# A fused attention, expert and gated network: the gated weights' preparation cut into three jobs, a step apart, behind the step's main operations

## The chip, the cores and the metric

The kernel runs on one core of a Trainium2 chip. The metric is the device time of one execution in microseconds (us); less is better. Given are three plain runs and one profiled execution of the kernel before.

## The reference

Three layers follow each other, all in float32 (shortened):

```python
# 1. attention with exponential features: 4 batches, 8 heads, 576 tokens, 64 wide
q_p, k_p = phi(q), phi(k)          # exp(+-(proj - max|proj|)), 2 x 128 features
x = (q_p @ (k_p.T @ v)) / (q_p @ sum(k_p) + 1e-6)      # then 2304 x 512
# 2. experts: 8, one for each token (the largest logit), gate weight = its softmax
h = np.maximum(x[mask] @ w1[e], 0.0)                   # 512 -> 1024
out[mask] = gate_w[mask, None] * (h @ w2[e])           # 1024 -> 512
# 3. gated layer: w_a, w_b 512 x 1536, w_out 1536 x 512
return (a * b @ w_out)             # a = x @ w_a, b = x @ w_b
```

The gated weights come to the device as 64-bit floats, each as two 32-bit words.

## The kernel before

The program is unrolled. A planner orders each engine's instructions when the program is built: it goes by priorities, by the dependencies and by its own costs for each operation. `high_priority(offset=-LOWP)` puts what is inside 200 places later in priority; `issue_after(ins)` lets what is inside follow `ins` on `ins`'s engine, in order and without a wait of its own. On the chip every engine runs its list in order, so an instruction that waits holds up all that is queued behind it. SyncE (SP) issues nearly all transfers, in order too.

The attention (class `Attn`) ends near 175 us in the profile. The expert stage (`Moe.run`) follows. The tokens come in two halves of 1152, each routed by itself (`Route`), and go in four tiles of 608 tokens. A tile has eight steps (`NJ`): in steps 0 to 3 two blocks each of the first layer (`l1`), in steps 4 to 7 one block each of the second (`l2`), so that the stage has 32 steps. TensorE multiplies each matrix in three products of high and low parts (`mm3`, L54 to L56), 304 columns at a time. An expert's weight block `s` is loaded, ScalarE rounds it to its high part `wh` (L552) and VectorE takes the low part `wl` (L553). Of the hidden layer ScalarE makes the high part `hh` (L591) and VectorE the low part `hl` (L592); both layers of matmuls need them, and the PSUM buffer of a block is free only when both have read it. GpSimd gathers token rows `xg` (L561), and TensorE turns them (`transp`).

At the start of step k, `run` calls what `side[k]` holds. Among it are the steps of the second half's routing (in steps 0, 2, 4, 8) and the preparation of ten of the twelve blocks of gated weights (`prep`, one block f at steps 3, 5, 8, 10, ... 25). The other two are prepared in the gated stage.

`prep` works on two halves of a block. For each half `narrow` loads the 64-bit words into `raw` (L688, two buffers), ScalarE takes the absolute value of the upper words (L692, tile `cvs`), GpSimd clamps it from below (L693), and VectorE builds the float32 in five instructions (L694 to L701) on `cvt`, `cvs` and, last, `wsum`. When both halves are there, VectorE makes four sums of column blocks (L710 to L713), ScalarE and VectorE split the block into a high part (`whi`, L718) and a low part (L719), in two cuts, and SyncE stores both in device memory (`wsc`, L720 and L721).

At step 28 `open_first` closes the pool of the preparation (`cctx`), opens in its room the pools of the gated stage, loads the first gated weights (`fw`, L730) and makes the first terms (`ysum`, `yl`). After the expert stage comes a branch that is not taken here, and then the gated stage (`Moe2.run`): 36 steps of seven products `abp` and six output accumulations each.

Of the kernel before, what the change touches and what calls it, by code (L numbers as in the profile page):

```python
# [48 lines left out]
def f32(ap):  # L49
    return ap.bitcast(F32)  # L50
# [283 lines left out]
class Route:  # L334
# [17 lines left out]
    def gate(self):  # L352
# [18 lines left out]
        ex = self.w([NG, E], "ex")  # L371
# [94 lines left out]
    def table(self):  # L466
# [19 lines left out]
        def lookup(name, col, n, row, parts):  # L486
            k = len(parts)
            hot = self.w([NG, n], name + "h", BF16)
            rhs = self.w([NG, k, n], name + "r", BF16)
# [30 lines left out]
class Moe:  # L520
# [26 lines left out]
    def splitw(self, T, j):  # L547
# [5 lines left out]
        nc.vector.tensor_sub(lo, src, f32(hi))  # L553
# [25 lines left out]
    def l1(self, T, f):  # L579
# [3 lines left out]
        for g in range(2):  # L583
            gs = slice(g * CG, g * CG + CG)
            for c in range(4):
# [5 lines left out]
        nc.scalar.activation(hh, ps[:, :, :CG], AF.Relu)  # L591
        nc.vector.scalar_tensor_tensor(out=hl, in0=ps[:, :, :CG], scalar=0.0, in1=f32(hh), op0=ALU.max,  # L592
                                       op1=ALU.subtract)
        T["h", f] = (hh, hl)

    def l2(self, T, m):
        nc = self.nc
        wh, wl = T["w", 4 + m]
        for g in range(2):
# [4 lines left out]
            nc.scalar.copy(self.y[T["rt"].bp][:, m, ds(T["s"][g], CG)], ps)  # L604
# [52 lines left out]
class Moe2:  # L657
# [14 lines left out]
    def pools(self, ctx, ps_a, ps_l):  # L672
# [3 lines left out]
        self.p_t[1] = pool("f_t1", 4)  # L676
# [4 lines left out]
    def narrow(self, pool, f, half, dst, nt):  # L681
        nc = self.nc
        n = 768
        if not self.f64:
            nc.sync.dma_start(out=dst, in_=self.w[f][:, n * half:n * half + n])
            return
        raw = pool.tile([P, n, 2], I32, tag="raw", name="raw", bufs=2)
        nc.sync.dma_start(out=raw.rearrange("p n w -> p (n w)"), in_=self.w[f][:, 2 * n * half:2 * n * half + 2 * n])  # L688
        lo, hi = raw[:, :, 0], raw[:, :, 1]
        t = pool.tile([P, n], I32, tag="t", name="cvt", bufs=nt)  # L690
        s = pool.tile([P, n], I32, tag="s", name="cvs", bufs=nt)
        nc.scalar.activation(s.bitcast(F32), hi.bitcast(F32), AF.Abs)  # L692
        nc.gpsimd.tensor_scalar(out=s.bitcast(F32), in0=s.bitcast(F32), scalar1=LEAST, scalar2=None, op0=ALU.max)  # L693
# [9 lines left out]
    def prep(self, f, pool, nw, nt):  # L703
        nc = self.nc
        w = pool.tile([P, 2304], F32, tag="w", name="wsum", bufs=nw)
        for half, c in enumerate((0, 1280)):
            self.narrow(pool, f, half, w[:, c:c + 768], nt)
# [6 lines left out]
        for x, y in self.CUTS:  # L714
# [6 lines left out]
            nc.sync.dma_start(out=self.wsc[f][1][:, x:y], in_=src)  # L721

# [169 lines left out]
def trn_kernel(ctx, tc, qk, v, vt, w_phi, mod_id, w_gate, bias, wm, wf, out):  # L892
# [37 lines left out]
    with ExitStack() as mctx:  # L930
# [27 lines left out]
        def conv(f):  # L958
            with tc.high_priority(offset=-LOWP):
                m2.prep(f, cv[0], 2, 2)  # L960

        K0, K1 = 3, len(tiles) * mo.NJ - 4
        for f in range(NPRE):
            side.setdefault(K0 + (K1 - K0) * f // NPRE, []).append(lambda f=f: conv(f))
# [90 lines left out]
```

## Time and profile before

| | us |
|---|---|
| plain runs: median (lowest to highest) of 3 | 829.94 (828.87 to 830.32) |
| profiled execution: time | 837.45 |
| profiled execution: span | 835.7 |
| TensorE busy in the span | 804.0 (96%) |
| VectorE busy | 595.1 (71%) |
| ScalarE busy | 373.8 (45%) |
| GpSimd busy | 140.4 (17%) |
| mean granted clock of TensorE | 0.991 |

The span goes from the first to the last instruction that the profile saw; the profiled execution's own time lies a little above it, and above the plain runs. Busy times are those of the profile's page; matmuls overlap, and their ends are modelled.

### The profile page before, as it was taken

Reading aid. Unit: us, or ns where it says so; the run is one execution under the profiler, and the core shown is the slowest. Engines: PE = TensorE matmul, PEld = TensorE weight load, DVE = VectorE, ACT = ScalarE, POOL = GpSimd, SP = SyncE. Lnnn points to the kernel's source line nnn. Section 1 sums busy time; section 2 is a strip of 40 time slices with the busy share of each in tenths; the row PEclk is TensorE's granted clock in tenths of the full one; section 3 lists DMA queues with packets and bytes.
Section 4 is the critical chain, followed back from the end, with each engine's and each line's share of the span. In section 5 each row is a group of like instructions: output and inputs, shape, how many; then the busy total and the mean of one; then the engine's idle time right before and its main releaser. Section 6 shows DMA issues by size and latency. Waiting matters only on the chain.

```text
span 835.7 us, 18329 instructions
## 1 busy us (share of the span) xinstructions
PE 804.0 (96%) x7283; PEld 755.5 (90%) x7284; DVE 595.1 (71%) x1071; ACT 373.8 (45%) x665; POOL 140.4 (17%) x164
## 2 busy tenths in 40 slices
PE   8999999889999999979999999999999999999996
PEld 6999888789999999979999899999999999999995
DVE  5888898589998999987488854775544676445553
ACT  3656555344544455453345433553333364333332
POOL 1000009342217433310021100030000002000002
PEclk9999999999999999999999999999999999999998
DMA  7666432466768888776499776576666568665632
GB/s 272 193 183 195 149 120 82 115 206 225 249 238 300 289 302 296 271 240 266 170 360 339 254 281 207 187 271 226 205 206 201 186 223 280 206 198 189 224 123 92
DMA packets 85163, 184.22 MB, mean 220 GB/s; under 512 B 27760, under 2 KB 37520, under 8 KB 85072
## 3 DMA queue, kind: packets, MB, share of 16 engines
q1 hardware_dynamic: 81872, 173.21, 61.4%
q0 software_dynamic: 3040, 9.72, 3.4%
q8 instruction: 58, 0.95, 0.5%
q14 instruction: 33, 0.27, 0.1%
q10 hardware_dynamic: 160, 0.07, 0.0%
HBM read 145.21 MB, written 37.75 MB: 219 GB/s over the span
## 4 chain that ended last, share of the span: by engine, by line
issue 44%; PE 4%; POOL 3%; POOLq 0%; ACT 0%
POOL out L800 2%; PE abp L54 1%; PE abp L56 1%; PE abp L55 1%; POOL cvs L693 1%; PE op L55 0%; PE op L54 0%; PE op L56 0%; POOLq L1052 0%; ACT cvs L692 0%; POOLq L800 0%; ACT pc L844 0%
## 5 line engine op out<-in xcount | busy, mean ns | idle before, releaser
L844 ACT COPY pc<-abp 128x384 f32<-128x384 f32 x252 | 120.6, 479 | 199.6 <-PE abp L56 195.9
L54 PE MATMUL abp<-yh,fw 128*128 128x384 f32 x504 | 170.1, 337 | 2.4 <-ACT pc L844 1.3
L56 PE MATMUL abp<-yh,fw 128*128 128x384 f32 x504 | 170.0, 337 | 0.0
L55 PE MATMUL abp<-yl,fw 128*128 128x384 f32 x504 | 169.8, 337 | 0.0
L54 PEld LDWEIGHTS abp<-yh,fw 128*128 128x128 f32 x504 | 94.6, 188 | 11.6 <-ACT pc L844 2.4
L55 PEld LDWEIGHTS abp<-yl,fw 128*128 128x128 f32 x504 | 94.7, 188 | 7.4
L693 POOL TENSOR_SCALAR cvs<-cvs 128x768 f32<-128x768 f32 x24 | 61.5, 2562 | 198.1 <-ACT cvs L692 184.4
L56 PEld LDWEIGHTS abp<-yh,fw 128*128 128x128 f32 x504 | 94.6, 188 | 0.0
L54 PE MATMUL hp<-mxh,wh 128*128 128x304 f32 x256 | 79.1, 309 | 7.9 <-DVE hl L592 6.8
L55 PE MATMUL op<-fw,gh 128*128 128x512 f32 x216 | 85.7, 397 | 0.0
L54 PE MATMUL op<-fw,gh 128*128 128x512 f32 x216 | 85.1, 394 | 0.0
L56 PE MATMUL op<-fw,gl 128*128 128x512 f32 x216 | 85.0, 394 | 0.0
L55 PE MATMUL yp<-hl,wh 128*128 128x304 f32 x256 | 77.3, 302 | 1.7 <-DVE hl L592 1.7
L55 PE MATMUL hp<-mxl,wh 128*128 128x304 f32 x256 | 78.2, 306 | 0.0
L56 PE MATMUL hp<-mxh,wl 128*128 128x304 f32 x256 | 77.8, 305 | 0.0
L56 PE MATMUL yp<-hh,wl 128*128 128x304 f32 x256 | 77.8, 304 | 0.0
L54 PE MATMUL yp<-hh,wh 128*128 128x304 f32 x256 | 76.9, 302 | 0.0
L800 POOL DMA_INDIRECT out<-o,perm x18 | 18.3, 1019 | 348.3 <-ACT o L799 341.2
L190 ACT ACTIVATE qts<-qtp 128x512 f32<-128x512 f32 (+1 forms) x80 | 38.3, 558 | 64.8 <-PE qtp L187 64.8
L855 DVE TENSOR_TENSOR d<-u,pc 128x768 f32<-128x768 f32 x36 | 34.5, 957 | 32.2 <-ACT pc L844 32.0
L54 PEld LDWEIGHTS hp<-mxh,wh 128*128 128x128 f32 x256 | 48.7, 190 | 9.4 <-issue 6.4
L156 DVE TENSOR_REDUCE m<-pjp 128x8 f32<-128x1024 f32 (+2 forms) x49 | 45.1, 933 | 12.0 <-PE pjp L154 12.0
(191 smaller groups left out, 1587.5 us busy)
## 6 DMA issues: line engine op xcount, KB each, us to landing
fw<-wsc SPq DMA_DIRECT2D x72, 512.0 KB, 5.4
fw<-wsc SPq DMA_DIRECT2D x144, 256.0 KB, 3.3
raw<-in_moe_w SPq DMA_DIRECT2D x24, 768.0 KB, 7.2
s<-in_moe_w SPq DMA_DIRECT2D x32, 512.0 KB, 4.2
fw<-wsc SPq DMA_DIRECT2D x72, 128.0 KB, 5.7
wsc<-whi SPq DMA_DIRECT2D x12, 640.0 KB, 4.3
wsc<-wsum SPq DMA_DIRECT2D x12, 640.0 KB, 6.8
wsc<-whi SPq DMA_DIRECT2D x12, 512.0 KB, 7.0
```

The source lines that it names most:

```text
L54: nc.tensor.matmul(out, lh, rh, start=start, stop=False)
L55: nc.tensor.matmul(out, lh, rl, start=False, stop=False)
L56: return nc.tensor.matmul(out, ll, rh, start=False, stop=stop).ins
L156: nc.vector.tensor_reduce(out=mv, in_=pv, op=ALU.max, axis=AX.X, apply_absolute_value=True)
L190: nc.scalar.activation(t[:, s, :n, :], ps[:, :n, :], AF.Exp, scale=1.0 - 2.0 * s)
L693: nc.gpsimd.tensor_scalar(out=s.bitcast(F32), in0=s.bitcast(F32), scalar1=LEAST, scalar2=None, op0=ALU.max)
L800: st = nc.gpsimd.indirect_dma_start(out=self.out[:, :], out_offset=bass.IndirectOffsetOnAxis(ap=self.routes[bp].perm[:, c:c + 1], axis=0), ...
L844: copied = nc.scalar.copy(x, ps).ins
L855: nc.vector.tensor_add(d, u, x.unsqueeze(1).to_broadcast([P, 2, n]))
```

## The change

The preparation is cut into three kinds of job. For each half of a block, `fetch` issues its raw transfer in step k, `clamp` lets ScalarE and GpSimd make `cvs` in step k + 1, and `narrow` lets VectorE build the float32 in step k + 2; behind the second half's `narrow` follow the sums, the split and the stores (`park`). Halves start at steps 2, 3, 4, 5, 6, 8, 9, ... 24, twenty of them, the gaps being 24/20 steps on average. All of a job is put behind the last main operations of the step before (`mo.act` on ScalarE: hh or the copy of the output; `mo.dve` on VectorE: hl or wl). `raw` has three buffers in place of two, `cvt` one in place of two. In the gated stage the two blocks left are prepared by the same jobs, a step apart, with two raw buffers as before. Room is found by sharing tags in the routing (`ex` with `bstmp`; the second half's `hot` and `rhs`) and by three in place of four buffers in `f_t1`.

```diff
         mx = self.w([NG], "mx")
         nc.vector.tensor_reduce(out=mx, in_=lg, op=ALU.max, axis=AX.X)
         nc.vector.tensor_sub(lg, lg, mx.unsqueeze(2).to_broadcast([P, NG, E]))
-        ex = self.w([NG, E], "ex")
+        ex = self.w([NG, E], "bstmp")
         nc.scalar.activation(ex, lg, AF.Exp)
         gt = self.gt = self.w([NG], "gt")
         nc.vector.tensor_reduce(out=gt, in_=ex, op=ALU.add, axis=AX.X)
...
 
         def lookup(name, col, n, row, parts):
             k = len(parts)
-            hot = self.w([NG, n], name + "h", BF16)
-            rhs = self.w([NG, k, n], name + "r", BF16)
+            hot = self.w([NG, n], "hot" if self.bp else name + "h", BF16)
+            rhs = self.w([NG, k, n], "rhs" if self.bp else name + "r", BF16)
             lhs = self.w([NG, P], "lhs" if self.bp else name + "l", BF16)
             onehot(hot, "icol", col, n)
             for i, v in enumerate(parts):
...
         hi = self.p_w.tile([P, 8, P], F32R, tag="h", name="wh")
         lo = self.p_w.tile([P, 8, P], F32R, tag="l", name="wl")
         nc.scalar.copy(hi, src)
-        nc.vector.tensor_sub(lo, src, f32(hi))
+        self.dve = nc.vector.tensor_sub(lo, src, f32(hi)).ins
         T["w", j] = (hi, lo)
 
     def gather(self, T, j):
...
                                 c == 0, c == 3)
         hh = self.p_h.tile([P, 2, CG], F32R, tag=f"h{f}", name="hh")
         hl = self.p_h.tile([P, 2, CG], F32R, tag=f"l{f}", name="hl")
-        nc.scalar.activation(hh, ps[:, :, :CG], AF.Relu)
-        nc.vector.scalar_tensor_tensor(out=hl, in0=ps[:, :, :CG], scalar=0.0, in1=f32(hh), op0=ALU.max,
-                                       op1=ALU.subtract)
+        self.act = nc.scalar.activation(hh, ps[:, :, :CG], AF.Relu).ins
+        self.dve = nc.vector.scalar_tensor_tensor(out=hl, in0=ps[:, :, :CG], scalar=0.0, in1=f32(hh), op0=ALU.max,
+                                                  op1=ALU.subtract).ins
         T["h", f] = (hh, hl)
 
     def l2(self, T, m):
...
             for f in range(8):
                 hh, hl = T["h", f]
                 self.last = mm3(nc, ps, wh[:, f, :], wl[:, f, :], hh[:, g, :], hl[:, g, :], f == 0, f == 7)
-            nc.scalar.copy(self.y[T["rt"].bp][:, m, ds(T["s"][g], CG)], ps)
+            self.act = nc.scalar.copy(self.y[T["rt"].bp][:, m, ds(T["s"][g], CG)], ps).ins
 
     def run(self, tiles, side={}):
         NT, NJ = len(tiles), self.NJ
...
         tc = self.tc
         pool = lambda n, b: ctx.enter_context(tc.tile_pool(name=n, bufs=b, side="right", reuse_waits="tile"))
         self.p_w[1] = pool("f_w1", 1)
-        self.p_t[1] = pool("f_t1", 4)
+        self.p_t[1] = pool("f_t1", 3)
         self.p_c = pool("f_c", 1)
         self.p_g = pool("f_g", 2)
         self.ps_a, self.ps_l = ps_a, ps_l
 
-    def narrow(self, pool, f, half, dst, nt):
+    def fetch(self, f, half, pool, n):
+        if not self.f64:
+            return None
+        c = 768 * 2
+        raw = pool.tile([P, 768, 2], I32, tag="raw", name="raw", bufs=n)
+        self.nc.sync.dma_start(out=raw.rearrange("p n w -> p (n w)"), in_=self.w[f][:, c * half:c * half + c])
+        return raw
+
+    def clamp(self, raw, pool, n):
+        if not self.f64:
+            return None
         nc = self.nc
-        n = 768
+        s = pool.tile([P, 768], I32, tag="s", name="cvs", bufs=n)
+        nc.scalar.activation(s.bitcast(F32), raw[:, :, 1].bitcast(F32), AF.Abs)
+        nc.gpsimd.tensor_scalar(out=s.bitcast(F32), in0=s.bitcast(F32), scalar1=LEAST, scalar2=None, op0=ALU.max)
+        return s
+
+    def narrow(self, f, half, raw, s, pool, w):
+        nc = self.nc
+        dst = w[:, 1280 * half:1280 * half + 768]
         if not self.f64:
-            nc.sync.dma_start(out=dst, in_=self.w[f][:, n * half:n * half + n])
+            nc.sync.dma_start(out=dst, in_=self.w[f][:, 768 * half:768 * half + 768])
             return
-        raw = pool.tile([P, n, 2], I32, tag="raw", name="raw", bufs=2)
-        nc.sync.dma_start(out=raw.rearrange("p n w -> p (n w)"), in_=self.w[f][:, 2 * n * half:2 * n * half + 2 * n])
         lo, hi = raw[:, :, 0], raw[:, :, 1]
-        t = pool.tile([P, n], I32, tag="t", name="cvt", bufs=nt)
-        s = pool.tile([P, n], I32, tag="s", name="cvs", bufs=nt)
-        nc.scalar.activation(s.bitcast(F32), hi.bitcast(F32), AF.Abs)
-        nc.gpsimd.tensor_scalar(out=s.bitcast(F32), in0=s.bitcast(F32), scalar1=LEAST, scalar2=None, op0=ALU.max)
+        t = pool.tile([P, 768], I32, tag="t", name="cvt")
         nc.vector.tensor_scalar(out=t, in0=s, scalar1=3, scalar2=0x3FFFFFF8,
                                 op0=ALU.logical_shift_left, op1=ALU.bitwise_and)
         nc.vector.scalar_tensor_tensor(out=t, in0=hi, scalar=-0x40000000, in1=t,
...
                                        in1=s.bitcast(F32), op0=ALU.mult, op1=ALU.mult)
         nc.vector.tensor_add(dst, t.bitcast(F32), s.bitcast(F32))
 
-    def prep(self, f, pool, nw, nt):
+    def sumw(self, pool, nw):
+        return pool.tile([P, 2304], F32, tag="w", name="wsum", bufs=nw)
+
+    def park(self, f, w, pool):
         nc = self.nc
-        w = pool.tile([P, 2304], F32, tag="w", name="wsum", bufs=nw)
-        for half, c in enumerate((0, 1280)):
-            self.narrow(pool, f, half, w[:, c:c + 768], nt)
         a11, a12, a21, s2, s1, a22 = (w[:, 256 * i:256 * i + 256] for i in range(6))
         s4 = w[:, 2048:]
         nc.vector.tensor_add(s1, a21, a22)
...
             nc.vector.tensor_sub(lo, src, f32(hi))
             nc.sync.dma_start(out=self.wsc[f][0][:, x:y], in_=f32(hi))
             nc.sync.dma_start(out=self.wsc[f][1][:, x:y], in_=src)
+
+    def jobs(self, f, pool, nw, nraw, ns):
+        st = {}
+
+        def fetch(half):
+            st["raw", half] = self.fetch(f, half, pool, nraw)
+
+        def clamp(half):
+            st["s", half] = self.clamp(st["raw", half], pool, ns)
+
+        def narrow(half):
+            if not half:
+                st["w"] = self.sumw(pool, nw)
+            self.narrow(f, half, st["raw", half], st["s", half], pool, st["w"])
+            if half:
+                self.park(f, st["w"], pool)
+
+        return fetch, clamp, narrow
 
     def weights(self, k):
         nc, f = self.nc, k % self.NF
...
         side = {k: [low(tc, rs[f])] for f, k in enumerate((0, 2, 4, 8))}
         side[9] = [close_work]
 
-        def conv(f):
-            with tc.high_priority(offset=-LOWP):
-                m2.prep(f, cv[0], 2, 2)
-
-        K0, K1 = 3, len(tiles) * mo.NJ - 4
+        def conv(f, half, job):
+            def run():
+                with tc.high_priority(offset=-LOWP), tc.issue_after(mo.act), tc.issue_after(mo.dve):
+                    job(half)
+            return run
+
+        K0, K1 = 2, len(tiles) * mo.NJ - 4
         for f in range(NPRE):
-            side.setdefault(K0 + (K1 - K0) * f // NPRE, []).append(lambda f=f: conv(f))
+            fetch, clamp, narrow = m2.jobs(f, cv[0], 2, 3, 2)
+            for half in range(2):
+                k = K0 + (K1 - 2 - K0) * (2 * f + half) // (2 * NPRE)
+                for i, job in enumerate((fetch, clamp, narrow)):
+                    side.setdefault(k + i, []).append(conv(f, half, job))
         ts, src0 = {}, []
 
         def first():
...
     cv.append(ctx.enter_context(tc.tile_pool(name="cv2", bufs=1, **tl)))
     side = {}
     for f in range(NPRE, Moe2.NF):
-        side.setdefault(2 * (f - NPRE), []).append(lambda f=f: m2.prep(f, cv[1], 1, 1))
+        for i, job in enumerate(m2.jobs(f, cv[1], 1, 2, 2)):
+            for half in range(2):
+                side.setdefault(2 * (f - NPRE) + i, []).append(lambda job=job, half=half: job(half))
     ps_l = ctx.enter_context(tc.tile_pool(name="ps_l2", bufs=2, space=PSUM, **tl))
     ps_a = ctx.enter_context(tc.tile_pool(name="ps_a2", bufs=1, space=PSUM, **tl))
     m2.pools(ctx, ps_a, ps_l)
```

## Rows read from the trace of the kernel before

**Rows 1.** Busy time by stretch (start:end, length; engine time and count; TensorE clock, DMA).

```profile
205.00:390.00 185.00, 176.89 (x1277) 175.35 (x1276) 165.98 (x264) 89.80 (x125) 60.71 (x26) 0.99 0.77 270
370.00:375.00 5.00, 1.42 (x8) 1.20 (x7) 5.00 (x7) 2.78 (x3) 0.00 (x0) 0.87 0.56 147
375.00:380.00 5.00, 5.00 (x31) 5.00 (x30) 4.48 (x6) 0.68 (x1) 0.00 (x0) 0.79 0.94 364
390.00:395.00 5.00, 5.00 (x38) 5.00 (x38) 4.55 (x6) 1.71 (x4) 0.00 (x0) 1.00 0.99 360
```

**Rows 2.** TensorE's timeline where it waited (start, length; idle before and releaser in brackets).

```profile
269.11 0.41 PE L55 MATMUL yp<-hl,wh 128*128 128x304 f32 x1 [1.74 <-DVE hl L592]
...
306.22 0.38 PE L54 MATMUL hp<-mxh,wh 128*128 128x304 f32 x1 [1.21 <-DVE hl L592]
...
360.32 0.41 PE L54 MATMUL hp<-mxh,wh 128*128 128x304 f32 x1 [1.58 <-DVE hl L592]
...
374.20 0.59 PE L54 MATMUL hp<-mxh,wh 128*128 128x304 f32 x1 [3.58 <-DVE hl L592]
...
410.20 0.44 PE L54 MATMUL abp<-yh,fw 128*128 128x384 f32 x1 [1.02 <-ACTq L983]
```

**Rows 3.** TensorE's waits from 415 us to the end.

```profile
PE abp L54 <- ACT pc L844: 1.3, 3, 0.8
```

**Rows 4.** VectorE's waits from 176 to 400 us.

```profile
DVE cvt L694 <- POOL cvs L693: 11.9, 5, 3.6
```

**Rows 5.** VectorE's timeline near three of TensorE's waits.

```profile
265.71 0.56 DVE L694 TENSOR_SCALAR cvt<-cvs 128x768 int32<-128x768 int32 x1 [3.56 <-POOL cvs L693]
...
350.83 0.56 DVE L694 TENSOR_SCALAR cvt<-cvs 128x768 int32<-128x768 int32 x1 [2.02 <-POOL cvs L693]
351.30 0.42 DVE L713 TENSOR_TENSOR wsum<-wsum 128x256 f32<-128x256 f32 x1
...
368.79 0.56 DVE L694 TENSOR_SCALAR cvt<-cvs 128x768 int32<-128x768 int32 x1 [2.45 <-POOL cvs L693]
...
373.28 1.48 DVE L592 SCALAR_TENSOR_TENSOR hl<-hp,hh 128x608 fp32r<-128x608 f32 x2
```

**Rows 6.** ScalarE's timeline before the longest wait.

```profile
365.64 0.91 ACT L692 ACTIVATE cvs<-raw 128x768 f32<-128x768 f32 x1 [5.94 <-DMA raw<-in_moe_w]
```

**Rows 7.** GpSimd's timeline, the clamp ahead of VectorE's wait at 265.71 us.

```profile
263.52 2.16 POOL L693 TENSOR_SCALAR cvs<-cvs 128x768 f32<-128x768 f32 x1
```

**Rows 8.** Transfers: issues, size, median us from issue to landing.

```profile
fw<-wsc SPq DMA_DIRECT2D x72, 512.0 KB, 5.4
...
raw<-in_moe_w SPq DMA_DIRECT2D x24, 768.0 KB, 7.2
```

**Rows 9.** SyncE's queue waits from 176 to 391 us.

```profile
SPq L688 <- DVE cvs L699: 18.9, 9, 5.7
```

**Rows 10.** Expert matmuls of the second layer: first and last start.

```profile
L54 PE MATMUL yp<-hh,wh x256: 296/300/391, 204.0 to 408.6; 128*128 128x304 f32 x128
```

**Rows 11.** VectorE's busy time 176 to 205 us on cvt, raw and wsum, in that order.

```profile
176.00:205.00 29.00, 9.35 (x13) 1.00 0.61 203
...
176.00:205.00 29.00, 5.68 (x6) 3.65 (x4) 1.00 0.61 203
...
176.00:205.00 29.00, 4.48 (x7) 1.06 (x1) 1.00 0.61 203
```

**Rows 12.** The rank of the second route: matmuls and the copy behind them.

```profile
L391 PE MATMUL rkp<-oh,ones x18: 166/188/203, 116.6 to 198.4; 128*128 128x72 bf16 x2, 128*128 128x64 bf16 x2, 128*128 128x56 bf16 x2, 128*128 128x48 bf16 x2
...
L394 DVE COPY R<-rkp x2: 226/233/240, 117.0 to 203.1; 128x80 f32<-128x80 f32 x2
```

**Rows 13.** VectorE's timeline: an instruction and the one that reads its result.

```profile
278.35 0.94 DVE L696 SCALAR_TENSOR_TENSOR cvt<-raw,cvt 128x768 int32<-128x768 int32 x1
279.32 0.56 DVE L698 TENSOR_SCALAR cvs<-cvt 128x768 int32<-128x768 int32 x1
```

**Rows 14.** SyncE's timeline: the first gated weights' loads.

```profile
391.84 20.56 SPq L730 DMA_DIRECT2D fw<-wsc  x13
```

## The prediction

> **What bounds the kernel now.** I first read the busy time by stretch, to see where TensorE can still gain anything. The change lives in the expert stage, which lies between about 176 and 410 us. In 205 to 390 us TensorE is busy 176.9 of 185 us and VectorE 166.0 [rows 1]. TensorE sets the pace, but VectorE is so full that one bad wait of its own is enough to hold TensorE up. The second view is TensorE's timeline at the places where it stood still: four times in this stretch, 1.74, 1.21, 1.58 and 3.58 us, together 8.1 us, and each time the releaser is hl, the low part of the hidden layer, which VectorE makes [rows 2]. The third is VectorE's list of waits: 11.9 us in five waits for GpSimd's clamp cvs [rows 4]. The timelines join the two: VectorE waits 3.56, 2.02 and 2.45 us for a clamp shortly before TensorE's waits at 269, 360 and 374 us; in the last case the two hl that TensorE needs start only at 373.28 [rows 5]. One step further back ScalarE, which feeds the clamp, had idled 5.94 us for the transfer raw [rows 6]. So the chain to read is transfer, ScalarE, GpSimd, VectorE, TensorE.
>
> After the longest wait the granted clock is 0.87 and 0.79 of full speed (2.4 GHz being full) for ten microseconds, and 31 matmuls start in 375 to 380 us where a free slice holds 38 [rows 1]: 7 x 5/38 = 0.9, call it 1.0 us. All that the expert stage can give back is thus 8.1 + 1.0 = 9.1 us. In the gated stage TensorE's waits are 1.3 us in all [rows 3]; nothing of size is to be had there.
>
> **What the change removes.** Before, a half's transfer, absolute value, clamp and arithmetic were queued together, with two raw buffers. The transfer for half i could start only when the arithmetic of half i-2 had read its buffer; SyncE stood 18.9 us on just that [rows 9]. VectorE needs about (166.0 + 13.8) / 20 = 9.0 us for one half together with the main work that falls in between (the 13.8 is worked out below). One half of lead is 9.0 us, and the way to the arithmetic takes 7.2 us for the transfer [rows 8], 0.91 on ScalarE [rows 6] and 2.16 on GpSimd [rows 7], 10.3 in all: it can't be hidden. With three buffers the lead is two halves, 18 us, and it is. The jobs also come a step apart, and a step is (408.6 - 204.0 - 9.1) / 28 = 7.0 us [rows 10], so ScalarE no longer stands in front of a transfer that has just been issued. I therefore take VectorE's waits for the clamp as gone where the raw transfer made the clamp late: TensorE's 1.58 and 3.58, and the 1.0 of clock, 6.2 us. I leave 1.21 in (no clamp wait stands before it), and 1.74 too: the clamp ahead of that one started on GpSimd with no idle time before it [rows 7], so it stood behind other work of GpSimd, the gathers of token rows, which the change doesn't move. The bounds are 0 (every wait is replaced by another) and 9.1.
>
> **What it moves.** The arithmetic of a half now stands behind the last VectorE operation of the step before it. The first such job is due in step 4, behind hl of step 3, so after about 205 us (the second layer, step 4, starts at 204.0 [rows 10]). Before, 13.8 us of preparation lay ahead of 205: 9.35 in 13 instructions on cvt, half of the 5.68 on raw (three of six, the product L699), and 4.48 less the three sums L701 already counted, some 1.6 [rows 11]. All that now falls into a stretch that is 166 of 185 us full. Something else may take its place: the second route's rank is done on TensorE at 198.4, its copy came only at 203.1 [rows 12], so VectorE can do part of the placing earlier; I take 3 us (0 to 5).
>
> VectorE then decides when the preparation ends: 205 + 166.0 + 13.8 - 3 = 381.8, plus its waits, plus what a serial order costs. Its waits are now 185 - 166 = 19 us; less those for the clamp after 205 us (8.0 in the three shown [rows 5], 11.9 in all five [rows 4]; I take 10), 9 stay (bounds 5 and 19). The single cvt buffer makes each half one chain: four links in it and two more per gate in the sums, 100 in all. An instruction that reads its neighbour's result starts 0.03 us after that one's end [rows 13], an unrelated neighbour starts 0.09 before it (the pair at 350.83 [rows 5]), so a link costs up to 0.12 us, 12 in all if nothing ever stands between. Of the 264 instructions in 205 to 390 us [rows 1] some 140 are preparation (ten gates of 16, less the 20 ahead of 205 [rows 11]), so there is nearly one other instruction for each; I take 5 us. The preparation then ends at 381.8 + 9 + 5 = 395.8.
>
> VectorE: DVE Perf Modes, in the Trainium skill (section The DRAIN you can't avoid), says that the next operation starts only when the pipeline has emptied and that a semaphore between chained operations adds nothing. By it a link would cost 0 and the preparation would end at 390.8; the pairs above differ by 0.12 us, and I keep the rows.
>
> What is late next is the first gated weights' load: it takes the room of the preparation's buffers and went out at 391.84 [rows 14], 1.8 us after the end of that stretch; 5.4 us later a load of 512 KB lands [rows 8]. So the gated stage can start 7.2 us after the preparation ends: at 403.0 by my sum. TensorE reaches it at 410.2 - 6.2 = 404.0, its 1.02 us at the branch included [rows 2]. The two limits lie 1 us apart, TensorE's being the later, and it counts. From 403.0 us on, every further microsecond of preparation would eat up the last of the gain: 403.0 + 7.2 = 410.2.
>
> **The other edits.** The transfers, clamps and stores are the same in number and size; on SyncE a fetch goes out earlier, ahead of stores that wait for ScalarE, and loads of expert weights stand behind it as before: 0, since the third buffer makes its wait [rows 9] shorter, and no wait of TensorE is put down to those loads [rows 2]. On GpSimd the clamp may still queue behind gathers; that is the 1.74 I left in. On ScalarE the absolute value (0.91 us) now stands behind the last main operation; main work queued behind it waits less than before (5.94 [rows 6]). ex in bstmp, shared hot and rhs: the second lookup's product now waits for the first lookup's matmuls; its lhs, one buffer already, did so next in line. 0, at worst one wait of VectorE like the longest seen, 3.56 [rows 5]. Three instead of four buffers in f_t1: two tiles a pass, and the one that is taken over was last read a whole step earlier; 0, or a wait of the size of those in rows 3. The last two gates' jobs in the gated stage: 0, at best part of that 1.3 us.
>
> **The sum.** 829.94 - 6.2 = 823.7 us. Times above are from the profiled execution, 837.45 us with a span of 835.7; it lies 7.5 us above the median of the plain runs (829.94), and I carry the difference over unchanged. A measurement can tell about 0.2%, 1.7 us, from no change.
>
> **Rivals.**
> *All of it.* The gathers' wait and the 1.21 go too, and VectorE ends by 394: 829.94 - 9.1 = 820.8. For it speaks that 18 us of lead covers even a clamp behind gathers; against it that VectorE must then take no more than 3 us for its links. 12%.
> *No change.* The preparation ends between 401 and 405 and the gated weights come just when TensorE used to need them; the waits are gone and the time is given back at the stage's end: 830. It needs 6 us more on VectorE than in my sum, half of what the bounds allow for links. 18%.
> *Slower.* The same place, beyond the point: the preparation ends after 403.0, because 13.8 us moved past 205 and the other waits stay. The bound is 205 + 166 + 13.8 + 12 + 19 = 415.8, the gated start 423.0. Halfway between 403.0 and that, 409.4, the start is 416.6, 6.4 us late, and with 1.0 us for the clock after such a pause the time is 837.3. For it speaks how full VectorE is; against it that 10 us of its waits have a cause that three buffers remove. 20%. By the skill's rule on links the bound would be 403.8, and this rival would have about half its chance.
> *My forecast*, 823.7, by itself 821.5 to 827: 50%.
>
> Faster by over 0.2% is then 0.62, within it 0.18, slower 0.20. The range runs from 819.5, just past the full 9.1, to 835.0, into the slower rival, whose far part (about one in ten) I leave out.
>
> **What the next profile would show.** Right: no preparation on VectorE before about 204 us; VectorE's waits for the clamp under 4 us; ScalarE's idle time for raw far below before; TensorE's waits at tile four (360 and 374 us) gone and the clock at full there; the gated stage starting near 404 us. Wrong: a load of gated weights as the releaser of the first gated matmul, or hl still behind preparation that waits for nothing, which would mean that VectorE's fullness and not its waits was what held TensorE.

## The result and the profile after

The changed kernel takes 841.9 us (840.8 to 844.8, four runs) where the kernel before took 829.8: the ratio is 1.0148, with an interval of 1.0115 to 1.0182. It is slower by about 12 us; 823.7 was forecast. The profiled execution took 842.58 us, with a span of 840.8.

The first view is the waits (total us, times, longest): TensorE's from 176 us to the end, and below them VectorE's from 176 to 400 us. They answer to [rows 2 to 4].

```profile
PE abp L54 <- DVEq L1019: 10.8, 1, 10.8
PE abp L54 <- ACT pc L874: 3.5, 5, 2.1
PE op L54 <- ACT gh L861: 1.6, 1, 1.6
PE op L56 <- DVE gl L862: 1.5, 1, 1.5
```

```profile
DVE wl L553 <- ACT wh L552: 7.5, 4, 2.8
DVE wsum L731 <- ACT whi L730: 5.7, 5, 2.8
DVE ysum L792 <- DMA wsc<-wsum: 4.2, 1, 4.2
DVE hl L592 <- ACT hh L591: 2.3, 2, 1.1
```

Two things are to be seen. What the change was to remove is gone: no wait of TensorE for hl is left, none of VectorE for the clamp cvs. But a single wait of 10.8 us has come, at the first gated matmul, and behind it 6.6 us in seven waits of the gated stage, where there were 1.3 [rows 3].

The busy time by stretch, of the changed kernel, answers to [rows 1]; columns as there.

```profile
176.00:205.00 29.00, 29.00 (x212) 28.37 (x211) 20.71 (x66) 11.00 (x15) 4.56 (x2) 1.00 0.44 143
205.00:390.00 185.00, 185.00 (x1351) 184.40 (x1350) 176.72 (x240) 95.04 (x131) 70.65 (x28) 1.00 0.76 273
...
395.00:400.00 5.00, 0.00 (x0) 0.00 (x0) 2.70 (x3) 0.14 (x2) 0.00 (x0) 0.72 0.36 104
400.00:405.00 5.00, 0.28 (x1) 0.31 (x2) 3.82 (x5) 3.01 (x4) 0.00 (x0) 0.50 0.99 365
405.00:410.00 5.00, 5.00 (x17) 5.00 (x17) 2.21 (x3) 2.27 (x4) 0.00 (x0) 0.50 0.34 103
```

From 205 to 390 us TensorE is busy all the time (176.9 before). Then it does nothing for ten microseconds, the granted clock falls to half, and only 17 gated matmuls start in 405 to 410 us. VectorE is at 176.7 of 185 us, and in 176 to 205 it was left idle for 8.3 of 29 us.

The rows of the second layer's matmuls and of VectorE's first conversion (shortest, median and longest in ns, first and last start):

```profile
L54 PE MATMUL yp<-hh,wh x256: 296/301/387, 199.0 to 393.3; 128*128 128x304 f32 x128
L706 DVE TENSOR_SCALAR cvt<-cvs x1: 547/547/547, 202.2 to 202.2; 128x768 int32<-128x768 int32 x1
```

VectorE's timeline where the stages meet (start, length; idle before and releaser in brackets):

```profile
390.68 1.49 DVE L731 TENSOR_TENSOR wsum<-wsum,whi 128x1280 fp32r<-128x1280 f32 x1 [2.77 <-ACT whi L730]
392.09 0.95 DVE L792 TENSOR_TENSOR ysum<-y 128x768 f32<-128x768 f32 x1
397.25 0.96 DVE L792 TENSOR_TENSOR ysum<-y 128x768 f32<-128x768 f32 x1 [4.22 <-DMA wsc<-wsum]
...
402.59 1.82 DVE L778 TENSOR_TENSOR yl<-ysum,yh 128x768 fp32r<-128x768 f32 x2
```

SyncE's timeline of the same place, and TensorE's:

```profile
392.19 0.32 SPq L733 DMA_DIRECT2D wsc<-wsum  x1
397.25 13.74 SPq L760 DMA_DIRECT2D fw<-wsc  x16
411.04 1.45 SPq L686 DMA_DIRECT2D raw<-in_moe_w  x2
```

```profile
404.72 0.66 PE L54 MATMUL abp<-yh,fw 128*128 128x384 f32 x1 [10.84 <-DVEq L1019]
405.18 0.52 PE L55 MATMUL abp<-yl,fw 128*128 128x384 f32 x1
405.50 0.52 PE L56 MATMUL abp<-yh,fw 128*128 128x384 f32 x1
```

The same place in the kernel before, on VectorE's timeline:

```profile
388.89 1.49 DVE L719 TENSOR_TENSOR wsum<-wsum,whi 128x1280 fp32r<-128x1280 f32 x1 [2.08 <-ACT whi L718]
...
410.18 0.96 DVE L762 TENSOR_TENSOR ysum<-y,ysum 128x768 f32<-128x768 f32 x1 [9.53 <-ACTq L983]
```

There the preparation ended at 390.4, 18.2 us before the last second-layer matmul started (408.6 [rows 10]), and VectorE, through with its block for the gated stage, waited 9.53 us for the branch.

In the changed kernel the preparation ends on VectorE at 392.2, 1.1 us before the last second-layer matmul starts. Everything of the gated stage that VectorE must still do (wait 4.2 us until the last prepared block is stored and its room free, then the terms ysum and the low parts yl, up to 404.4) comes behind it. TensorE waits for VectorE to reach the branch (DVEq). The weights' load goes out at 397.25 for the same reason, and 16 of its transfers stand ahead of the first raw transfer of the gated stage.

**Three lengths for every kernel.** The attention takes a different time in every execution, so I measure from the first second-layer matmul (yp), as three lengths: *layer*, from there to the start of the last yp; *gap*, from there to the first gated matmul; *gated*, from there to the end of the span. "Preparation ends" is the end of the last low part (wsum of wsum and whi), also counted from the first yp. All of it comes from the start times shown as in the rows above, in one profiled execution each; the ratios come from repeated runs and stand against the kernel before run in the same set on the same chip (medians 829.4, 833.7, 828.5 and 834.9 us in the four sets below, on chips numbered 14, 2, 2 and 12).

| kernel | ratio | preparation ends | layer | gap | gated | sum |
|---|---|---|---|---|---|---|
| before | 1 | 186.4 | 204.6 | 1.6 | 425.5 | 631.7 |
| e1, before again | 0.9998 | 181.9 | 200.1 | 1.6 | 425.6 | 627.3 |
| after | 1.0148 | 193.2 | 194.3 | 11.4 | 436.1 | 641.8 |
| e12, after again | 1.0111 | 193.1 | 194.3 | 10.1 | 436.3 | 640.7 |
| e2, gated jobs of before | 1.0048 | 193.1 | 194.3 | 10.0 | 430.7 | 635.0 |
| e3, gated jobs alone | 0.9990 | 184.1 | 202.4 | 1.6 | 424.5 | 628.5 |
| e4, no pins | 0.9908 | 183.1 | 195.9 | 1.6 | 424.7 | 622.2 |
| e5, VectorE's pin alone | 1.0087 | 194.8 | 194.4 | 12.9 | 429.2 | 636.5 |
| e6, ScalarE's pin alone | 1.0059 | 191.9 | 194.4 | 8.5 | 431.1 | 634.0 |
| e7, two steps earlier | 1.0010 | 188.6 | 194.4 | 5.7 | 431.6 | 631.7 |
| e8, no pins, two raw | 0.9956 | 187.1 | 196.3 | 2.3 | 426.9 | 625.5 |
| e9, TensorE kept busy | 1.0073 | 193.0 | 194.3 | 10.1 | 431.9 | 636.3 |
| e10, nine blocks | 0.9867 | 180.6 | 194.9 | 1.6 | 424.8 | 621.3 |
| e11, weights' room first | 1.0071 | 193.4 | 194.4 | 10.6 | 433.1 | 638.1 |
| e13, before, nine blocks | 0.9932 | 163.7 | 196.9 | 1.6 | 424.7 | 623.2 |
| e14, no pins, nine blocks | 0.9897 | 166.9 | 195.5 | 1.6 | 424.9 | 622.0 |

The sum less 629.5 (the mean of the two executions of before) gives the measured change of the time (from the ratio, times 830) within 3 us in every row: +12.3 for after (12.1 measured), -7.3 for e4 (-7.6), -8.2 for e10 (-11.0). The three lengths thus hold what differs.

### The profile page after: what moved, and what is told of

The parts are those of the page before. It is cut to its first block, busy times and chain, and to the rows that moved or that the text cites. A ratio compares the mean times of both kernels' runs of the same rounds, so it can differ in the third digit from the quotient of the medians.

```text
span 840.8 us, 18335 instructions
## 1 busy us (share of the span) xinstructions
PE 804.9 (96%) x7283; PEld 757.1 (90%) x7284; DVE 603.9 (72%) x1071; ACT 376.2 (45%) x665; POOL 146.3 (17%) x164
## 4 chain that ended last, share of the span: by engine, by line
PE 26%; issue 16%; DVE 4%; DMA 2%; POOL 1%; ACT 1%; SPq 0%; POOLq 0%; DVEq 0%; ACTq 0%
PE abp L54 6%; PE abp L56 6%; PE abp L55 6%; PE op L55 3%; PE op L54 3%; PE op L56 3%; POOL cvs L695 1%; DMA raw<-in_moe_w 1%; DMA wsc<-whi 1%; DMA wsc<-wsum 1%; ACT pc L874 0%; POOL out L830 0%; DVE cvt L708 0%; DVE ca L860 0%; SPq L760 0%
## 5 line engine op out<-in xcount | busy, mean ns | idle before, releaser
L874 ACT COPY pc<-abp 128x384 f32<-128x384 f32 x252 | 120.5, 479 | 206.1 <-PE abp L56 202.4
L54 PE MATMUL abp<-yh,fw 128*128 128x384 f32 x504 | 172.0, 341 | 14.3 <-DVEq L1019 10.8
L54 PEld LDWEIGHTS abp<-yh,fw 128*128 128x128 f32 x504 | 95.9, 190 | 24.1 <-issue 11.1
L695 POOL TENSOR_SCALAR cvs<-cvs 128x768 f32<-128x768 f32 x24 | 67.6, 2820 | 169.6 <-ACT cvs L694 153.0
L56 PEld LDWEIGHTS abp<-yh,fw 128*128 128x128 f32 x504 | 95.8, 190 | 0.0
L156 DVE TENSOR_REDUCE m<-pjp 128x8 f32<-128x1024 f32 (+2 forms) x49 | 45.1, 933 | 12.1 <-PE pjp L154 12.1
L861 ACT CAST gh<-ca 128x384 fp32r<-128x384 f32 x72 | 36.8, 514 | 35.9 <-DVE ca L860 35.9
```

What stands on the lines that cost most here:

```text
L54: nc.tensor.matmul(out, lh, rh, start=start, stop=False)
L56: return nc.tensor.matmul(out, ll, rh, start=False, stop=stop).ins
L156: nc.vector.tensor_reduce(out=mv, in_=pv, op=ALU.max, axis=AX.X, apply_absolute_value=True)
L861: nc.scalar.copy(gh, ca[:, i, :])
L874: copied = nc.scalar.copy(x, ps).ins
```

## The experiments

"Pins" are the two `issue_after` that put a job behind the last main operations of the step before.

**Parts of the change, first set.** e1 is the kernel before once more.

> The kernel before, unchanged, for a second profile. First theory: the profiled execution of before (837.45 us) lay 7.5 us above its plain runs because it had waits that plain runs don't have; a new profile then lies near 830 us, with TensorE's waits in the expert stage well under the 8.1 us counted before. Rival: profiling adds a constant, and the new profile shows about 837 us and the same waits of 3.6, 1.7, 1.6 and 1.2 us.

Measured: ratio 0.9998 (0.9967 to 1.0028), but a span of 825.4 us where the first profile had 835.7. TensorE's waits in the expert stage:

```profile
PE hp L54 <- DVE hl L592: 3.5, 4, 1.9
```

That is less than half of [rows 2], with a longest wait of 1.9 in place of 3.58. The execution on which I had built the sum was a long one; its 7.5 us above the plain runs were no fixed offset, and its waits no fixed amount.

e2 keeps the changed expert stage and queues the gated stage's two blocks all at once, as before.

```diff
-        for i, job in enumerate(m2.jobs(f, cv[1], 1, 2, 2)):
+        fetch, clamp, narrow = m2.jobs(f, cv[1], 1, 2, 1)
+        for half in range(2): for job in (fetch, clamp, narrow): ... at step 2 * (f - NPRE)
```

> The kernel after, but in the gated stage all of a block's preparation is queued at once as before, with one clamp buffer. First theory: about 5 us of the loss are the gated stage's own waits (2.1 us at 419, 1.6 and 1.5 at 446 and 448, and the clock after them), made by the jobs' new places there: 837 us (835.5 to 838.5). Rival: the gated stage's jobs are innocent and the whole loss is the late start with the cold clock: 842 us.

Measured: 1.0048 (1.0020 to 1.0076); the gap is still 10.0, but the gated stage is 5.4 us shorter than that of after.

e3 is the reverse: an expert stage with the jobs of a block queued at once, unpinned, with two raw and two cvt buffers; only the gated stage has the new jobs.

```diff
-                with tc.high_priority(offset=-LOWP), tc.issue_after(mo.act), tc.issue_after(mo.dve):
+                with tc.high_priority(offset=-LOWP):
...
-            fetch, clamp, narrow = m2.jobs(f, cv[0], 2, 3, 2)
+            fetch, clamp, narrow = m2.jobs(f, cv[0], 2, 2, 2)   # all at one step
```

> The new functions and the room they need, the expert stage's preparation queued at once with two raw and two cvt buffers as before, and only the gated stage's jobs a step apart. First theory: 830 + 5 = 835 us (833 to 836.5). Rival: 830 us.

Measured: 0.9990 (0.9959 to 1.0022), gated stage 424.5. The 5 us of loss that I expected didn't come: the jobs of the gated stage cost nothing behind a start in time, and 5.4 us (e2) behind the late start of after. e3 also keeps the shared tags and the three buffers in `f_t1`, so these cost nothing that its interval could show.

e4 is the changed kernel without the pins; the jobs stay a step apart and low in priority.

```diff
-                with tc.high_priority(offset=-LOWP), tc.issue_after(mo.act), tc.issue_after(mo.dve):
+                with tc.high_priority(offset=-LOWP):
```

> The kernel after without the rule that puts the preparation behind the last main operations of the step before; jobs still a step apart, three raw buffers. First theory: VectorE starts on the preparation some 20 us earlier, as before, ends it 10 us or so before 392, and the gated stage starts without a long pause: 832 us (829 to 835). Rival: what makes the preparation end late is its serial order with one cvt buffer; it still ends near 390 and the time is 840 to 843 us.

Measured: 0.9908 (0.9878 to 0.9938), faster than before, and by more than the best that I expected (829). Busy time by stretch of e4:

```profile
176.00:205.00 29.00, 27.36 (x197) 26.23 (x196) 29.00 (x51) 15.29 (x21) 11.13 (x4) 1.00 0.71 232
```

VectorE is busy for all of the first 29 us (20.7 with the pins): the first conversion comes at 173.2 in place of 202.2, which is 22.0 us before the first yp in place of 3.2 behind it. The preparation ends 10.1 us sooner, the gap is gone, and TensorE's layer is 195.9, nearly as short as with the pins. e4 and after differ in the pins alone: the pins turn the gain into a loss.

**Which pin, and how late; second set.** e5 keeps only VectorE's pin, e6 only ScalarE's.

> The kernel after with the rule kept on VectorE alone (the absolute value on ScalarE is free). First theory: it is VectorE's late start that costs, so nothing comes back: 840 us (836 to 843), first narrow instruction on VectorE at 200 us or later, the preparation's last store after 388. Rival: ScalarE's part of the rule holds the clamps back and with them all else: 821 to 826 us.

> The kernel after with the rule kept on ScalarE alone. First theory: the first clamp comes only after the hidden block of step 2 (about 191 us), so VectorE still starts some 15 us later than without the rule, but later jobs are free: between the two, 828 us (823 to 834). Rival: the rule on VectorE is all: 821 us, as without any rule.

Measured: 1.0087 (1.0049 to 1.0125) and 1.0059 (1.0027 to 1.0091). First conversions at 206.7 and 201.8, which is 3.3 us behind the first yp and 3.2 before it; preparation 194.8 and 191.9. Either pin by itself makes the start late against e4's 22.0 before, since the conversion needs ScalarE's result too. Of e6 I had expected a ratio near 0.998 (828 us); nearly all of the loss stayed.

e7 keeps both and lets the first half start at step 0 (`K0 = 0`).

> The kernel after, rule and all, with the first fetch in step 0 in place of 2 (the first narrow in step 2, the same last step). First theory: VectorE gains about two steps of 6.7 us, the preparation ends 10 us or so earlier, near 382, TensorE's pause before the gated stage falls under 3 us, the clock stays full: 824 us (821 to 829). Rival: the rule's order itself fills VectorE (chains with nothing between), so the end moves little: 836 us or more.

Measured: 1.0010 (0.9991 to 1.0028), where the 824 expected would be 0.993. The first conversion came 12.0 us before the first yp, the preparation ended 4.6 us earlier than in after, and the gap fell to 5.7: the direction is right, but 15 us earlier at the front are worth only a third of that at the end.

e8 is e4 with two raw buffers.

> Without the rule, and with two raw buffers in place of three; jobs still a step apart. First theory: the third buffer is what keeps VectorE from waiting for the clamp; without it TensorE's waits in the expert stage come back in part, 825 us (823 to 828). Rival: the jobs' spacing does it and the third buffer nothing: 821 us.

Measured: 0.9956 (0.9929 to 0.9983). ScalarE's waits for the transfer in e8, 176 to 400 us:

```profile
ACT cvs L694 <- DMA raw<-in_moe_w: 44.2, 17, 5.9
```

In e4 they are 3.5 us in one. Yet TensorE's layer is 196.3 against 195.9: TensorE's waits go without the third buffer too, with the jobs a step apart. With the buffer the preparation ends 4.0 us sooner; about half of e4's gain goes with it, though the two intervals meet and the chips differ.

**What the pause costs, third set.** e12 is the changed kernel again.

> The changed kernel as it is, on the chip of the three others: a second profile of it, for what repeats. Theory: ratio to the kernel before near 1.015; TensorE pauses 9 to 12 us ahead of the first gated matmul, VectorE's first conversion comes near 202 us, the granted clock falls to its lower level in the first 10 us of the gated stage, and a gated stage some 8 to 11 us longer than that of the kernel before. Rival (the first profile of it was one slow execution): pause under 6 us and ratio under 1.008.

Measured: 1.0111 (1.0090 to 1.0132), and the pause is there again; the row is TensorE's wait in e12:

```profile
PE abp L54 <- DVEq L1019: 9.5, 1, 9.5
```

e9 adds matmuls that nothing reads behind the last second-layer matmul (40 in the code, 80 on TensorE).

```diff
+        hold, ident = ps_t.tile([P, 512], F32, tag="t", name="hold"), cst["ident"]
+        with tc.issue_after(mo.last):
+            for i in range(NHOLD):
+                nc.tensor.matmul(hold[:, :P], ident, ident, start=i == 0, stop=i == NHOLD - 1)
```

> The changed kernel with 40 extra fp32 matmuls of the 128x128 identity on TensorE right behind the last second-layer matmul, into a PSUM tile that nothing reads; they fill the pause of 10.8 us before the first gated matmul. Theory (the pause costs its own length and then the half clock that follows it): the first gated matmul starts when it did, but its stage runs at the full clock, about 2.7 us shorter and with the waits for pc smaller, so 837 to 840 where the changed kernel has 842. Rival (the half clock costs nothing since the first gated matmuls would wait for splits of VectorE anyway): 842, no change; should the extra matmuls outlast the pause, slower than 842.

Measured: 1.0073 (1.0053 to 1.0094), 2.9 us less than e12 on the same chip. TensorE's timeline of e9:

```profile
391.83 8.09 PE L1023 MATMUL hold<-ident 128*128 128x128 f32 x71
400.49 0.41 PE L55 MATMUL abp<-yh,fw 128*128 128x384 f32 x1 [0.56 <-PEq L1024]
400.74 0.34 PE L56 MATMUL abp<-yl,fw 128*128 128x384 f32 x1
400.91 0.34 PE L57 MATMUL abp<-yh,fw 128*128 128x384 f32 x1
```

(The row shows 71 of the 80.) The gap is the same 10.1 us, but the first gated matmuls begin 0.17 us apart and not 0.32. Keeping TensorE busy gives back 2.9 us in the plain runs, and the gated stage of the profile is 4.4 us shorter. The clock isn't full for all of it: 6.0 us of waits for pc remain, and behind the longest, 3.55 us, gated matmuls begin 0.32 us apart again.

e11 changes only addresses: the pool of the gated weights is opened ahead of those of the terms, so it no longer lies on the last prepared block.

```diff
+            m2.p_w[0] = ctx.enter_context(tc.tile_pool(name="f_w0", bufs=1, **tl))
             m2.p_t[0] = ...; m2.p_s = ...
-            m2.p_w[0] = ctx.enter_context(tc.tile_pool(name="f_w0", bufs=1, **tl))
```

> The changed kernel with only an address changed: the room of the first gated weights (fw) is opened ahead of the temporary tiles, so that it no longer lies where the last wsum block was. Theory (fw's load waits 5 us for that block's store to land, while VectorE's first ysum waits 4.2 us for the same store): the load goes out up to 4 us earlier; if VectorE's ysum and splits still wait for their own room the first gated matmul gains less, 0 to 4 us, so 838 to 842 where the changed kernel has 842. Rival (the store's landing holds only the load, and VectorE's splits set the start): no change.

Measured: 1.0071 (1.0043 to 1.0099), 3.8 us less than e12 by the medians (the intervals meet), but not where expected. SyncE's and VectorE's timelines of e11:

```profile
390.38 14.06 SPq L760 DMA_DIRECT2D fw<-wsc  x14
```

```profile
388.49 1.49 DVE L731 TENSOR_TENSOR wsum<-wsum,whi 128x1280 fp32r<-128x1280 f32 x1 [2.77 <-ACT whi L730]
391.60 1.83 DVE L792 TENSOR_TENSOR ysum<-y 128x768 f32<-128x768 f32 x2 [1.62 <-DMA wsc<-whi]
394.99 0.96 DVE L778 TENSOR_TENSOR yl<-y,yh 128x768 fp32r<-128x768 f32 x1 [1.56 <-DMA wsc<-wsum]
...
401.61 0.96 DVE L792 TENSOR_TENSOR ysum<-y,ysum 128x768 f32<-128x768 f32 x1 [0.33 <-DVEq L1019]
```

The load goes out 0.4 us after the preparation's end (3.8 in e12), and still the gated stage starts 11.6 us after that end (11.2). So not the load but VectorE's own block of terms sets the start; in e11 too 3.2 us of that block are waits for stores to leave its room. The gated stage is 3.2 us shorter instead, with 4.9 us of waits of TensorE in place of 6.7; that the load then stands less in the way of the first raw transfers is argued, not shown.

e10 prepares nine blocks in the expert stage, and three in the gated stage (`NPRE = 9`).

> The changed kernel with nine blocks of gated weights prepared in the expert stage in place of ten, three left to the gated stage. Theory (VectorE's preparation ends late, and one block is about 9 us of VectorE with its spacing): the last split ends about 8 us earlier relative to the second-layer matmuls, the pause falls from 10.8 us to 2 to 4, the clock is not halved for long, and the time is 0.990 to 1.000 of the kernel before. Rival (what the kernel lost lies in the gated stage, which now has a block more to prepare): ratio 1.010 or more.

Measured: 0.9867 (0.9847 to 0.9887), the lowest ratio of all and better than the 0.990 to 1.000 expected. The preparation ends 12.6 us sooner than in after (8 expected), and at the joint VectorE's timeline of e10, and then TensorE's, read:

```profile
378.46 1.49 DVE L731 TENSOR_TENSOR wsum<-wsum,whi 128x1280 fp32r<-128x1280 f32 x1 [1.22 <-ACT whi L730]
384.11 1.83 DVE L792 TENSOR_TENSOR ysum<-y 128x768 f32<-128x768 f32 x2 [4.15 <-DMA wsc<-wsum]
390.49 1.82 DVE L778 TENSOR_TENSOR yl<-ysum,yh 128x768 fp32r<-128x768 f32 x2
395.87 0.96 DVE L792 TENSOR_TENSOR ysum<-y,ysum 128x768 f32<-128x768 f32 x1 [3.56 <-ACTq L1019]
```

```profile
395.89 0.44 PE L54 MATMUL abp<-yh,fw 128*128 128x384 f32 x1 [1.03 <-ACTq L1019]
```

The wait of 4.15 us for the store and the block of terms are still there, but VectorE is through by 392.3 and then idles 3.56 us for the branch, where in after TensorE waited for VectorE. The gated stage with three blocks is as long as with two, 424.8.

**Whose gain is it? Fourth set.** e13 is the kernel before with nine blocks, e14 is e4 with nine.

> The kernel before with nine blocks of gated weights prepared in the expert stage in place of ten, nothing else. Theory (the kernel before is bound by TensorE in the expert stage, its preparation ends some 18 us ahead of TensorE, and one block less takes nothing off the path, while the gated stage has one more): ratio 0.997 to 1.003, so the gain of nine blocks in the changed kernel belongs to the change's steps. Rival (ten blocks were too many for any order, and the gain is that of nine alone): ratio 0.985 to 0.990, as the changed kernel with nine blocks.

> The changed kernel without the pins behind the main operations, and nine blocks in place of ten. Theory (without the pins the preparation ended in time with ten blocks already, so one block less saves no wait): ratio 0.988 to 0.993, that of the changed kernel without the pins. Rival (a VectorE less crowded is worth something by itself, or the gated stage pays for the block): 0.984 or less, or 0.996 or more.

Measured: 0.9932 (0.9905 to 0.9959) and 0.9897 (0.9868 to 0.9926). For e13 I was wrong: nine blocks speed up the kernel before too, by 0.7%. Its layer is 196.9, and TensorE's waits for hl are 2.8 us (8.5 and 3.5 in the two profiles with ten blocks): here a VectorE with less to do held TensorE less. So part of e10's 1.3% isn't the change's. Against nine blocks in the kernel before, the changed kernel with nine gains 0.65% (0.9867 / 0.9932, on different chips). e14 came as the theory had it, equal to e4 within the intervals: once the preparation ends in time, taking away more of it saves nothing. Whether pins or none are better with nine blocks stays open (0.9867 and 0.9897, intervals that overlap, different chips).

## Why the prediction was wrong, step by step

By the lengths above, the forecast for the profiled execution was: first yp at 204.0, layer 198.4 (204.6 - 6.2), gap 1.6, gated 425.5. Measured were 199.0, 194.3, 11.4 and 436.1. With the offset of 7.5 us, which was 0.7, the differences are -5.0, -4.1, +9.8, +10.6 and +6.8, together 18.1 of the 18.2 us by which the forecast failed.

- *TensorE's waits go, for 6.2 us*: right in kind. All are gone; the layer went from 204.6, or 200.1 in the second execution, to 194.3, which is 10.3 or 5.8 us: more than forecast by the execution on which the sum was built, and about as forecast by the other. The cause that I gave, the third buffer, isn't needed for it: e8 shows the layer nearly as short with two raw buffers and 44.2 us of ScalarE's waits for the transfer.
- *The preparation ends at 395.8*, 191.8 after the first yp: measured 193.2, but by errors that cancel. The sum counts from 1.0 us behind the first yp, in after from 200.0; from there to the end VectorE's busy time reads:

```profile
200.00:392.20 192.20, 192.20 (x1402) 191.60 (x1401) 183.24 (x253) 97.62 (x135) 73.06 (x29) 1.00 0.75 267
```

That is 183.2 us where the sum has 166.0 + 13.8 - 3 = 176.8, and 9.0 us idle where it has 14 for waits and links. One part of the surplus can be read: the 160 preparation instructions, added up one by one, took 130.8 us in after and 124.2 before (131.0 in e4); why was not tried. The links were kept at 5 us by the rows; the prediction's reading of VectorE: DVE Perf Modes in the Trainium skill (section The DRAIN you can't avoid) put the end at 186.8. That section also says that a next operation that isn't held starts earlier, and the trace agrees: the neighbour at 351.30 [rows 5] started 0.09 us before the end of the one at 350.83. So the section doesn't rule out that a link costs something against independent work. No run measured the links alone.
- *What is late next is the weights' load, 7.2 us behind the preparation*: **this step failed.** What is late next is VectorE itself, with the terms ysum and yl queued behind the preparation: the start came 12.5 us after its end in after, and 11.0 to 12.5 in all eight others that have a gap over 1.6 us, 11.6 in e11 with a load that went out at once. Before, VectorE did the same block under TensorE's last matmuls (the lines above). With some 11.4 us the preparation must end (194.3 + 1.6) - 11.4 = 184.5 us after the first yp, not 192.8 as in my sum (404.0 - 7.2 - 204.0). Of the table, e3, e4, e10, e13 and e14 end before it and have no gap; all the others that have the short layer end after it and have one.
- *The gated stage is as long as before*: **the second step that failed**, and as dear: 10.6 us. Two things that can be read for every late kernel nearly add up to it: TensorE's waits in the gated stage beyond the 1.3 us of before, and the clock, as each 2 us slice's length times the part of full speed that wasn't granted (an estimate from the profiles' slices; 0 in both profiles of before). I had 1.0 of clock, and only in the rival.

| kernel | gap | waits beyond 1.3 | clock | both | gated beyond 425.5 |
|---|---|---|---|---|---|
| after | 11.4 | 5.3 | 4.8 | 10.1 | 10.6 |
| e12, after again | 10.1 | 5.4 | 5.3 | 10.7 | 10.8 |
| e9, TensorE kept busy | 10.1 | 4.7 | 1.7 | 6.4 | 6.4 |
| e2, gated jobs of before | 10.0 | 1.8 | 3.6 | 5.4 | 5.2 |
| e5, VectorE's pin alone | 12.9 | 1.1 | 2.2 | 3.3 | 3.7 |

  For e6, e7, e8 and e11 the two come within 0.9 us as well. So the price isn't fixed by the gap: e5 has the longest gap and the same gated jobs, and pays 3.7. What makes the waits longer in after than in e5 was not tried. Two of after's can be followed. The first: SyncE issues the raw transfer at 411.04, behind 16 of the late weights' load; the absolute value waits for it, and the copy pc for which TensorE stands still is queued behind it (ScalarE's and TensorE's timelines):

```profile
418.02 0.89 ACT L694 ACTIVATE cvs<-raw 128x768 f32<-128x768 f32 x1 [1.72 <-DMA raw<-in_moe_w]
418.81 0.47 ACT L874 COPY pc<-abp 128x384 f32<-128x384 f32 x1
```

```profile
419.33 0.45 PE L54 MATMUL abp<-yh,fw 128*128 128x384 f32 x1 [2.11 <-ACT pc L874]
```

  The second: at 446 us TensorE waits for gh and gl, and behind these waits its matmuls start 0.32 us apart again. gl stands on VectorE behind the low part of a block that the gated stage prepares itself (TensorE's and VectorE's timelines):

```profile
445.87 0.50 PE L54 MATMUL op<-fw,gh 128*128 128x512 f32 x1 [1.59 <-ACT gh L861]
...
448.13 0.55 PE L56 MATMUL op<-fw,gl 128*128 128x512 f32 x1 [1.53 <-DVE gl L862]
448.48 0.53 PE L54 MATMUL abp<-yh,fw 128*128 128x384 f32 x1
448.80 0.53 PE L55 MATMUL abp<-yl,fw 128*128 128x384 f32 x1
```

```profile
446.13 1.48 DVE L731 TENSOR_TENSOR wsum<-wsum,whi 128x1280 fp32r<-128x1280 f32 x1
447.53 1.01 DVE L862 TENSOR_TENSOR gl<-ca,gh 128x384 fp32r<-128x384 f32 x2
```

- *The offset of 7.5 us, carried over unchanged*: wrong, but the first yp came 5.0 us earlier, so the two together cost 1.8 us. The profiled execution of before was a long one: in e1's the first yp came 5.9 us earlier and the layer was 4.5 us shorter. That the early yp and the lost offset nearly cancel is luck.
- *The rivals.* The slower one named the right place and a fair time (837.3), though by the wrong next link, and got 20%. The sign to look for, a load as the releaser of the first gated matmul, didn't come: the releaser is VectorE's queue.
- *What I didn't see*: that the pins make the loss (e4 against after). Moving 13.8 us of VectorE's work past 205 us was in my sum; that the same jobs without the pins would begin at 173 us was not asked.

## What to carry to other kernels

When background work is moved on a nearly full engine, work out not only when it ends but everything that this engine must still do behind it for the next stage; the trace of before showed that block, and the change took away its cover. A late start can cost more than its own length: behind gaps of 10.0 to 12.9 us the gated stage was 3.7 to 10.8 us longer, by the clock and by waits. A pin that holds low-priority work back from an idle stretch buys order with the very slack that the work was to fill; take the pin away, or a block of the work, before giving up the change.

## What was unexpected of the hardware

- After TensorE had stood still for 5.1 to 12.3 us (e7, e5), the granted clock was near 0.50, the lower of its two levels (1.2 GHz), and gated matmuls began 0.32 us apart in place of 0.17. In after that lasted 5.9 us from the restart, for 18 of them. The same slow starts also followed shorter waits in the gated stage: 2.39 us for pc in e12, 2.63 in e2, 3.55 in e9, and in after 1.59 and 1.53 us with two matmuls between them. They didn't follow the 2.11 us for pc in after, nor the 1.8 us of e8. In e9, with matmuls that nothing reads in the pause, the gated stage ran at full clock up to the 3.55 us.
- Executions of the same program differ well ahead of the change: the first second-layer matmul came at 204.0 and at 198.1 us in two profiles of the kernel before, at 199.0 and at 194.5 in two of the changed one. Whether the chip makes the difference was not tried.
- GpSimd's clamp of 128x768, 2.16 us in [rows 7], took up to 5.03 us in the kernel before and up to 8.09 us in the changed one; what stretched it was not tried.
